# Attention ahead of two feed-forward layers: the order of its last steps, banks for the second queries, and the place of the block means

## The chip, the cores and the metric

The kernel runs on one core of a Trainium2 chip. The metric is the device time of one execution in microseconds (us); a run's time is compared by the median of several executions. Engines: PE multiplies matrices (PEld loads its weights), DVE, ACT and POOL work elementwise, SP issues the DMAs. Each engine runs its own list of instructions strictly in order and waits on semaphores for the others.

## What is computed

Three layers follow each other. The first is attention with 2 x 8 heads, 768 positions of 64 numbers, in which a query sees the keys nearer than 16 positions and, for each block of 32 positions, one summary (the maximum of the keys, the mean of the values):

```python
k_sum = k.reshape(B, H, nb, block, D).max(axis=3)
v_sum = v.reshape(B, H, nb, block, D).mean(axis=3)
scores_l = np.where(abs(i - j) < 16, scale * q @ k.T, -1e9)
scores_s = scale * q @ k_sum.T + np.log(block)
a = softmax(concatenate([scores_l, scores_s]))
x = a @ concatenate([v, v_sum])
x = (lambda h: h * np.cos(h))(x @ w_in) @ w_out          # 1536 x 512 -> 2048 -> 512
out = layernorm(h * softmax(h)) * g_ln @ w_out2          # h = x @ w_in2, 1024 wide
```

## The kernel before

The inputs are float32, or float64 read as pairs of words; here the weights come as pairs and are turned into float32 on the chip. Products of the feed-forward layers run in three passes over a high and a low part of each operand, so each weight tile is split into w[:, 0] and w[:, 1], and each input tile X into xs.

**Attention.** Heads go in 8 pairs n, each pair in 3 groups, 24 groups G = 3n + g of 4 query tiles of 64. One loop of 29 steps (L614) runs a software pipeline over the groups, and each engine's list is simply the order in which the loop emits: scores s(G) one step ahead (PE, L510, one bank for even and one for odd G), maximum and mask max(G) on DVE (L521), subtraction on POOL (L525), exp(G) a step later on ACT (L530), sum on DVE (L534), norm(G) two steps later on POOL (L540), the transposes T(G) of the weights four steps later on PE (L547, bank 2), their copy at(G) on ACT, or on DVE for the last four groups (L555, L553), the product with the values av(G) on PE (L567, bank 3), and x(G), the copy of its result into X (L581 on ACT, L579 on DVE from group 19 on). Even and odd steps are mirrored: av runs for two groups in every even step (L639), x for two groups in every odd step (L665).

**Pairs.** k(n) and q(n) are loaded by SP (L357; 384 KB each), set side by side (L375), transposed on PE into one tile of three banks (L443, L482), from which DVE takes the maximum of each key block, ksum (L455), and ACT copies the keys, kx (L464 to L474), and the queries, qx (L496). The first queries q(0) go to banks 2 and 3 and DVE copies them (L492). v(n) comes by four DMAs (L389, L393; 2 x 240 and 2 x 48 KB). vsum(n) on PE (L421) adds up each block of values, ACT scales the sums to means, vm(n) (L429), and SP places them by two DMAs into the rows of the v tile that av reads (L436). VSUM_AT says at which step vsum(n) stands, VLOAD_AT at which v(n) is loaded; the placing stood at the end of the step after vsum's, behind that step's loads (L688 to L694).

**Into the next layer.** While the attention runs, SP loads weights (raw, L139; 512 KB), and ACT and DVE (L163, L164, L171), then ACT and POOL (L186, L187) turn them into w. From step 15 on, FILL puts 48 products h of the first feed-forward layer (L234) between the attention's instructions on PE: four tiles h(0) to h(3). drain(k) emits what h needs behind it: u (ACT, L243), n (DVE, L248), sin (ACT, L253), h*r (DVE, L258), and the split gs (ACT L263, DVE L264). After the loop come the splits of X (L203, L204), then the products y(0), y(1) (L276) and from there an even alternation of h and y.

Of the kernel before, what the change touches and what calls it, by code (L numbers as in the profile page):

```python
# [34 lines left out]
def fused_kernel(  # L35
# [14 lines left out]
    nc = tc.nc  # L50
# [43 lines left out]
    WSTEPS = (4, 7, 10, 13, 16, 19, 20, 21)  # L94
    XS = (7, 11, 13, 17)
    IDLE = (0, 0, 0)
    DVE_AT = 20
    DVE_X = 19
    DVE_NORM = 99
    LAST = 5  # L100
# [205 lines left out]
            nc.tensor.matmul(t, lhsT=idle[:, 0:P], rhs=idle, start=True, stop=True)  # L306


    FILL = {15: 3, 16: 3, 17: 3, 18: 3, 20: 4, 21: 4, 22: 4, 23: 4, 24: 4, 25: 4, 26: 4, 27: 4, 28: 4}
    early = (x for step in range(GF) for x in h_products(step))  # L310

    def fill(step):
# [8 lines left out]

        nc.scalar.activation(out=small[:, 1:2], in_=small[:, 0:1], func=func)

    STAGES = ((emit_sin, 2), (emit_r, 2), (emit_u, 1), (emit_n, 1), (emit_g, 2))

    def drain(k):

        if k == 0:
            table(AF.Sin)
        for stage, at in STAGES:  # L330
            if 0 <= k - at < GF and (stage, k - at) != (emit_g, GF - 1):
                stage(k - at)


    def attention():
        st = ExitStack()
        with st:
# [24 lines left out]
            def load_q(n):  # L362
                q_t[n] = load_heads(q, n, "qt", NR)

            def load_k(n):
                k_t[n] = load_heads(k, n, "kt", 2)
# [17 lines left out]
            def load_v(n):  # L384
                b, hp = divmod(n, NP)
                t = io.tile([P, NT, 2, D], F32, tag="vt", name="vt", bufs=5)
                for j in range(2):
                    o = v[b, 2 * hp + j].offset
                    nc.sync.dma_start(  # L389
                        out=t[0:WIN, 1:NT - 1, j, :],  # L390
                        in_=bass.AP(v.tensor, o + (QT - BAND) * D, [[D, WIN], [QT * D, NT - 2], [1, D]]),
                    )
                    nc.sync.dma_start(  # L393
                        out=t[0:WIN, 0:NT:NT - 1, j, :],
                        in_=bass.AP(v.tensor, o, [[D, WIN], [(S - WIN) * D, 2], [1, D]]),
                    )
                v_t[n] = t
# [77 lines left out]
                    out=kx[:, :, WIN:KW], in_=ks_t.pop(n).unsqueeze(1).to_broadcast([P, NT, NS]), func=AF.Copy)  # L475

            def emit_q(n):
                if n == 0:
                    qk_t["q", n] = bank(2, "q0"), bank(3, "q1")
                t, (a, b) = q_t.pop(n), qk_t["q", n]  # L480
                for c in range(NR):
                    nc.tensor.transpose(  # L482
                        (a, b)[c // (NR // 2)][:, (c % (NR // 2)) * P:(c % (NR // 2) + 1) * P],
                        t[:, c].rearrange("p h d -> p (h d)"), ident)

            def emit_qx(n):
                qx = io.tile([P, S], F32, tag="qx", name="qx")
                rows = qx.rearrange("p (i r) -> p i r", r=NR)
                src = qk_t.pop(("q", n))
                if n == 0:  # L490
                    for r in range(2):
                        nc.vector.tensor_scalar_mul(  # L492
                            rows[:, :, r * NR // 2:(r + 1) * NR // 2],
                            src[r][:, 0:S // 2].rearrange("p (r i) -> p i r", i=P), 0.125)
                else:
                    nc.scalar.activation(  # L496
                        out=rows, in_=strided(src[0], 0, [[1, P], [P, NR]]), func=AF.Copy, scale=0.125)
                kx_t["q", n] = qx
# [50 lines left out]

            def emit_at(G):  # L550
                at = sm_p.tile([KW, NG, P], F32, tag="at", name="at", bufs=3)
                if G >= DVE_AT:
                    nc.vector.tensor_copy(at, at_t[G])  # L553
                else:
                    nc.scalar.activation(out=at, in_=at_t[G], func=AF.Copy)  # L555
                at_t[G] = at

            def emit_av(G):
                n, g = divmod(G, GPP)
                b, hp = divmod(n, NP)  # L560
                at, vt = at_t.pop(G), v_t[n]
                if G % 2 == 0:
                    o_t["bank"] = bank(3, "ops").rearrange("p (a i s) -> p a i s", a=2, i=NG)
                ops = o_t["bank"][:, G % 2]
                for i in range(NG):
                    for j in range(2):
                        nc.tensor.matmul(  # L567
                            ops[64 * j:64 * j + 64, i, :], lhsT=vt[0:KW, NG * g + i, j, :],
                            rhs=at[:, i, 64 * j:64 * j + 64], start=True, stop=True)
                o_t[G] = ops  # L570
# [17 lines left out]
            nc.sync.dma_start(out=mask.rearrange("p t k -> p (t k)"), in_=c_mask)  # L588
            load_k(1)
            load_q(1)  # L590
            load_k(2)
            load_q(2)
            load_v(0)
            nc.gpsimd.memset(small, 0.0)
            nc.gpsimd.memset(strip, 0.0)
            warm_up(8)
# [12 lines left out]


            LX, LN, LT, LA = 1, 2, 4, 5
            VSUM_AT = {3: 0, 4: 1, 7: 2, 9: 3, 12: 4, 13: 5, 16: 6, 19: 7}
            VLOAD_AT = {1: 1, 4: 2, 6: 3, 8: 4, 10: 5, 13: 6, 16: 7}
            for step in range(NGR + LA):  # L614
                n, g = divmod(step, GPP)
                summed = LN <= step < NGR + LN
                ahead = 1 if step == 1 else n + 1 if g == 0 and 0 < n < NPAIR - 1 else 0

                warm_up(IDLE[g] if step < min(FILL) else 0)
                odd = step % 2  # L620
                if step + 1 < NGR and not odd:
                    emit_s(step + 1)
                if odd and step in VSUM_AT:
                    sum_v(VSUM_AT[step])
                if step == 0:
                    pair_k(1)
                    emit_max(0)
                    pair_q(1)
                    emit_k(1)
                    emit_q(1)  # L630
                if LT <= step < NGR + LT:
                    emit_t(step - LT)
                if g == 2 and n + 2 < NPAIR:
                    emit_k(n + 2)
                    emit_q(n + 2)
                fill(step)
                if odd and step + 1 < NGR:
                    emit_s(step + 1)
                if not odd and step > LA:  # L639
                    emit_av(step - LA - 1)  # L640
                    emit_av(step - LA)
                if not odd and step in VSUM_AT:
                    sum_v(VSUM_AT[step])

                weights.split()
                if LX <= step < NGR + LX:
                    emit_exp(step - LX)
                if g == 1 and 0 < n < NPAIR - 1:
                    emit_kx_ends(n + 1)
                if summed:  # L650
                    emit_sum(step - LN)
                if ahead and step > 1:
                    emit_ksum(ahead)
                weights.rebias()
                if 0 < step < NGR:
                    emit_max(step)
                if step == 1:
                    emit_ksum(ahead)
                drain(step - NGR)
                if LT <= step < NGR + LT:  # L660
                    emit_at(step - LT)
                weights.finish()
                if summed:
                    emit_norm(step - LN)
                if step > LA and (odd or step == NGR + LA - 1):  # L665
                    end = step - LA + 1 - odd
                    emit_x(end - 2)
                    emit_x(end - 1)
                if ahead:
                    emit_kx(ahead)  # L670
                if step == 1:
                    emit_kx_ends(1)
                if step == 0:
                    emit_qx(1)
                if g == 2 and n + 2 < NPAIR:
                    emit_qx(n + 2)
                if step == 2:
                    weights.load(0)
                if step in WSTEPS:
                    weights.bits()  # L680
                for c in range(KC):
                    if step == XS[c]:
                        xs_of[0, c] = split_x(0, c, xs_a)
                if g == 1 and n + 2 < NPAIR:
                    pair_k(n + 2)
                    pair_q(n + 2)

                if g == 1 and n + 3 < NPAIR:  # L688
                    load_k(n + 3)
                    load_q(n + 3)  # L690
                if step in VLOAD_AT:
                    load_v(VLOAD_AT[step])
                if step - 1 in VSUM_AT:
                    place_vsum(VSUM_AT[step - 1])  # L694
                if step in VSUM_AT:
                    scale_v(VSUM_AT[step])

    with tc.manual_schedule():
# [200 lines left out]

        for c in range(KC):  # L900
            xs_of[1, c] = split_x(1, c, xs_b, nc.vector if c % 2 else nc.gpsimd)
        for k in range(LAST, 7):
            drain(k)
        emit_y(0)
        emit_y(1)
        for step in range(4, NSTEP):
# [93 lines left out]
```

## Time and profile before

| what | us |
|---|---|
| median of 3 runs | 493.17 (493.09 to 496.96) |
| the profiled execution | 493.84 |
| its span, first to last instruction | 492.0 |
| PE busy | 474.6 (96%) |
| ACT, DVE, POOL busy | 313.5, 302.7, 152.3 |

Only the span is profiled; 1.84 us of the profiled execution lie outside it. In a timeline row, the number behind the start is the duration, x8 is a count, and the bracket at the end says how long the engine had been idle before and which instruction ended that. fp32 products of the attention appear as two instructions each, so x16 is eight of the code's products. PEclk is TensorE's granted clock, 1.00 for 2.4 GHz.

### The profile page before, as it was taken

Reading aid. Unit: us, or ns where it says so; the run is one execution under the profiler, and the core shown is the slowest. Engines: PE = TensorE matmul, PEld = TensorE weight load, DVE = VectorE, ACT = ScalarE, POOL = GpSimd, SP = SyncE. Lnnn points to the kernel's source line nnn. Section 1 sums busy time; section 2 is a strip of 40 time slices with the busy share of each in tenths; the row PEclk is TensorE's granted clock in tenths of the full one; section 3 lists DMA queues with packets and bytes.
Section 4 is the critical chain, followed back from the end, with each engine's and each line's share of the span. In section 5 each row is a group of like instructions: output and inputs, shape, how many; then the busy total and the mean of one; then the engine's idle time right before and its main releaser. Section 6 shows DMA issues by size and latency. Waiting matters only on the chain.

```text
span 492.0 us, 7874 instructions
## 1 busy us (share of the span) xinstructions
PE 474.6 (96%) x2943; PEld 392.2 (80%) x2943; DVE 302.7 (62%) x666; ACT 313.5 (64%) x539; POOL 152.3 (31%) x146
## 2 busy tenths in 40 slices
PE   7789998899999999999999999999999999999997
PEld 4678877678888888888888888888888888888886
DVE  3698885783445446556474655556477766776661
ACT  2579877756686666656655653688624867777621
POOL 2388978722432223222322220245500011110000
PEclk9899999999999999999999999999999999999999
DMA  8888973201322332232223220220001333223211
GB/s 256 233 176 240 239 177 103 87 2 37 93 85 87 109 105 87 86 118 98 87 88 117 95 86 25 87 105 0 0 2 43 87 87 85 65 64 65 68 40 43
DMA packets 59046, 46.17 MB, mean 94 GB/s; under 512 B 40448, under 2 KB 51328, under 8 KB 59008
## 3 DMA queue, kind: packets, MB, share of 16 engines
q1 hardware_dynamic: 59008, 45.67, 32.5%
q8 instruction: 23, 0.38, 0.3%
q14 instruction: 15, 0.12, 0.1%
HBM read 36.61 MB, written 3.15 MB: 81 GB/s over the span
## 4 chain that ended last, share of the span: by engine, by line
PE 84%; ACT 4%; POOL 3%; DVE 3%; DMA 3%; issue 2%; SPq 1%; POOLq 0%; DVEq 0%; ACTq 0%
PE y L276 27%; PE h L234 24%; PE o L875 13%; PE h L761 13%; PE vsum L421 2%; POOL sm L525 1%; PE sps L510 1%; DMA qt<-in_q_dram 1%; POOL sm L540 1%; DMA vt<-in_v_dram 1%; PE aps L547 1%; PE ops L567 1%; ACT sm L530 1%; PE tp L809 1%; DMA vt<-vm 1%
## 5 line engine op out<-in xcount | busy, mean ns | idle before, releaser
L234 PE MATMUL h<-xs,w 128*128 128x512 f32 x576 | 141.2, 391 | 0.4 <-POOL xs L204 0.4
L276 PE MATMUL y<-gs,w 128*128 128x512 f32 x576 | 138.2, 389 | 0.0
L276 PEld LDWEIGHTS y<-gs,w 128*128 128x128 f32 x576 | 108.1, 188 | 22.5
L234 PEld LDWEIGHTS h<-xs,w 128*128 128x128 f32 x576 | 107.3, 188 | 22.3 <-POOL xs L204 0.7
L187 POOL TENSOR_TENSOR w<-s,w 128x512 fp32r<-128x512 f32 x48 | 62.1, 1295 | 155.8 <-ACT w L186 132.8
L243 ACT ACTIVATE r<-h 128x512 int32<-128x512 f32 x48 | 28.7, 597 | 85.7 <-PE h L234 85.7
L248 DVE SCALAR_TENSOR_TENSOR r<-r,h 128x512 f32<-128x512 int32 x48 | 33.0, 687 | 67.8 <-ACT r L243 67.6
L875 PE MATMUL o<-w,ls 128*128 128x512 f32 (+1 forms) x312 | 67.8, 374 | 0.0
L761 PE MATMUL h<-w,xs 128*128 128x512 f32 x288 | 67.6, 390 | 0.0
L171 DVE SCALAR_TENSOR_TENSOR s<-raw 128x512 int32<-128x512 int32 x48 | 37.1, 774 | 45.9 <-ACT raw L164 38.1
L875 PEld LDWEIGHTS o<-w,ls 128*128 128x128 f32 x312 | 55.3, 188 | 10.7 <-DVE ls L851 0.4
L761 PEld LDWEIGHTS h<-w,xs 128*128 128x128 f32 x288 | 53.9, 188 | 11.1
L204 POOL TENSOR_TENSOR xs<-X,xs 128x512 fp32r<-128x512 f32 x22 | 29.6, 1355 | 36.9 <-ACT xs L203 36.9
L796 POOL TENSOR_TENSOR st<-st,mhalf 128x1 f32<-128x1 f32 x12 | 6.6, 551 | 110.1 <-DVE st L795 101.7
L264 DVE TENSOR_TENSOR gs<-h,gs 128x512 fp32r<-128x512 f32 x48 | 32.7, 680 | 4.2 <-ACT gs L263 4.0
L253 ACT ACTIVATE r<-r,half_pi 128x512 f32<-128x512 f32 x48 | 34.5, 718 | 1.0 <-DVE r L248 1.0
L258 DVE TENSOR_TENSOR h<-h,r 128x512 f32<-128x512 f32 x48 | 32.9, 686 | 0.4 <-ACT r L253 0.4
L163 ACT ACTIVATE raw<-raw 128x512 f32<-128x512 f32 x48 | 31.9, 664 | 0.0
L164 ACT ACTIVATE raw<-raw 128x512 int32<-128x512 uint32 x48 | 31.8, 662 | 0.0
L186 ACT ACTIVATE w<-s 128x512 fp32r<-128x512 f32 x48 | 30.1, 628 | 1.8 <-DVE s L171 1.5
L525 POOL TENSOR_TENSOR sm<-sm,mx 128x480 f32<-128x480 f32 x24 | 26.0, 1083 | 15.2 <-DVE mx L521 15.2
L778 ACT ACTIVATE e<-h,st 128x1024 f32<-128x1024 f32 (+1 forms) x13 | 13.6, 1049 | 26.6 <-DVE st L774 23.2
(81 smaller groups left out, 560.4 us busy)
## 6 DMA issues: line engine op xcount, KB each, us to landing
raw<-in_moe_w_in_dram SPq DMA_DIRECT2D x24, 512.0 KB, 3.6
raw<-in_moe_w_out_dram SPq DMA_DIRECT2D x24, 512.0 KB, 3.3
vt<-in_v_dram SPq DMA_DIRECT2D x16, 240.0 KB, 5.8
kt<-in_k_dram SPq DMA_DIRECT2D x8, 384.0 KB
qt<-in_q_dram SPq DMA_DIRECT2D x8, 384.0 KB, 8.9
out_dram<-osb SPq DMA_DIRECT2D x11, 256.0 KB, 2.0
vt<-vm SPq DMA_DIRECT2D x16, 72.0 KB
vt<-in_v_dram SPq DMA_DIRECT2D x16, 48.0 KB, 4.5
```

Source lines behind the costliest of these rows:

```text
L163: nc.scalar.activation(out=hw, in_=hw, func=AF.Prelu, scale=REBIAS, alpha=NEGATIVE)
L164: nc.scalar.activation(out=lw, in_=lw.bitcast(U32), func=AF.Copy, scale=TOP3)
L171: nc.vector.scalar_tensor_tensor(out=self.f32[i], in0=t[:, :, 1], scalar=3, in1=t[:, :, 0], op0=ALU.logical_shift_left, op1=ALU.bitwise_or)
L187: nc.gpsimd.tensor_tensor(out=w[:, 1, :], in0=f, in1=as32(w[:, 0, :]), op=ALU.subtract)
L234: nc.tensor.matmul(h, lhsT=w[:, a, f * P:(f + 1) * P], rhs=xs_of[tb, c][:, b_, :], start=(m == 0), stop=(m == 3 * KC - 1))
L248: nc.vector.scalar_tensor_tensor(out=r, in0=r.bitcast(I32), scalar=TWO_PI, in1=h_of[step], op0=ALU.mult, op1=ALU.subtract)
L253: nc.scalar.activation(out=r, in_=r, func=AF.Sin, scale=-1.0, bias=half_pi)
L258: nc.vector.tensor_tensor(out=h, in0=h, in1=r, op=ALU.mult)
L264: nc.vector.tensor_tensor(out=gs[:, 1, :], in0=r, in1=as32(gs[:, 0, :]), op=ALU.subtract)
L276: nc.tensor.matmul(y[e], lhsT=w[:, a, e * P:(e + 1) * P], rhs=gs[:, b_, :], start=(f == 0 and i == 0), stop=(f == GF - 1 and i == 2))
L761: nc.tensor.matmul(banks[n], lhsT=xs_of[NTB + t // TPB, c][:, a, t0:t0 + P], rhs=weights.done[w2i[c][n]][:, b_, :], start=(m == 0), stop=( ...
L875: nc.tensor.matmul(o, lhsT=ls_of[t][f // 4][:, a, s0:s0 + P], rhs=w[:, b_, cols], start=(f == 0 and i == 0), stop=(f == NF2 - 1 and i == 2))
```

## The change

Seven edits, all in the attention and in what it overlaps with.

1. q(1) goes to banks 2 and 3 like q(0), and DVE copies it, in step 1 behind ksum(1).
2. v(0) is loaded ahead of k(2) and q(2), and vsum(0) stands in step 2 instead of 3.
3. The placing of vm(n) is emitted at the start of the step after vsum's, ahead of that step's loads.
4. FILL begins at step 16 instead of 15, and vsum(7) stands behind s(20) in step 19.
5. From step 24 on the steps are alike: av of one group in each, x of the same group at its end. av(20) to av(23) each use the first half of bank 3.
6. at stays on ACT for all groups and is emitted ahead of drain.
7. drain follows a table: u and n of h(0) and h(1) in steps 22 and 23, the others by the table, u, n, sin and h*r of h(3) after the loop.

```diff
-    FILL = {15: 3, 16: 3, 17: 3, 18: 3, 20: 4, 21: 4, 22: 4, 23: 4, 24: 4, 25: 4, 26: 4, 27: 4, 28: 4}
+    FILL = {16: 3, 17: 3, 18: 3, 19: 3, 20: 4, 21: 4, 22: 4, 23: 4, 24: 4, 25: 4, 26: 4, 27: 4, 28: 4}
...
-    STAGES = ((emit_sin, 2), (emit_r, 2), (emit_u, 1), (emit_n, 1), (emit_g, 2))
+    DRAIN = {
+        -2: ((emit_u, 0), (emit_n, 0)),
+        -1: ((emit_u, 1), (emit_n, 1)),
+        1: ((emit_sin, 0), (emit_r, 0)),
+        2: ((emit_sin, 1), (emit_r, 1), (emit_g, 0), (emit_u, 2), (emit_n, 2)),
+        3: ((emit_sin, 2), (emit_r, 2), (emit_g, 1)),
+        4: ((emit_g, 2),),
+        5: ((emit_u, 3), (emit_n, 3), (emit_sin, 3), (emit_r, 3)),
+    }
...
             def emit_q(n):
-                if n == 0:
+                if n < 2:
                     qk_t["q", n] = bank(2, "q0"), bank(3, "q1")
...
-                if n == 0:
+                if n < 2:
                     for r in range(2):
                         nc.vector.tensor_scalar_mul(
...
-                if G >= DVE_AT:
-                    nc.vector.tensor_copy(at, at_t[G])
-                else:
-                    nc.scalar.activation(out=at, in_=at_t[G], func=AF.Copy)
+                nc.scalar.activation(out=at, in_=at_t[G], func=AF.Copy)
...
-                if G % 2 == 0:
+                if G % 2 == 0 or G >= NGR - LT:
                     o_t["bank"] = bank(3, "ops").rearrange("p (a i s) -> p a i s", a=2, i=NG)
-                ops = o_t["bank"][:, G % 2]
+                ops = o_t["bank"][:, G % 2 if G < NGR - LT else 0]
...
             load_q(1)
+            load_v(0)
             load_k(2)
             load_q(2)
-            load_v(0)
...
-            VSUM_AT = {3: 0, 4: 1, 7: 2, 9: 3, 12: 4, 13: 5, 16: 6, 19: 7}
+            VSUM_AT = {2: 0, 4: 1, 7: 2, 9: 3, 12: 4, 13: 5, 16: 6, 19: 7}
...
+                if step - 1 in VSUM_AT:
+                    place_vsum(VSUM_AT[step - 1])
                 odd = step % 2
                 if step + 1 < NGR and not odd:
                     emit_s(step + 1)
-                if odd and step in VSUM_AT:
+                if odd and step in VSUM_AT and step < 19:
                     sum_v(VSUM_AT[step])
...
-                if not odd and step > LA:
+                if not odd and LA < step <= NGR:
                     emit_av(step - LA - 1)
+                if LA < step and (not odd or step > NGR):
                     emit_av(step - LA)
-                if not odd and step in VSUM_AT:
+                if step in VSUM_AT and (not odd or step == 19):
                     sum_v(VSUM_AT[step])
...
-                drain(step - NGR)
                 if LT <= step < NGR + LT:
                     emit_at(step - LT)
+                drain(step - NGR)
...
-                if step > LA and (odd or step == NGR + LA - 1):
-                    end = step - LA + 1 - odd
-                    emit_x(end - 2)
-                    emit_x(end - 1)
+                if LA < step < NGR and odd:
+                    emit_x(step - LA - 2)
+                    emit_x(step - LA - 1)
+                if step == NGR:
+                    emit_x(step - LA - 1)
+                if step >= NGR:
+                    emit_x(step - LA)
...
-                if step - 1 in VSUM_AT:
-                    place_vsum(VSUM_AT[step - 1])
```

Three places in the engines' lists. SP, steps 2 to 5, before: the first two weight loads, then k(4), q(4) and v(2), and behind them the placing of v(0) and v(1) together.

```order
L139 DMA raw<-in_moe_w_in_dram 128x1024 x2
L357 DMA kt<-in_k_dram 128x6x128
L357 DMA qt<-in_q_dram 128x2x384
L389 DMA vt<-in_v_dram 96x10x64
L393 DMA vt<-in_v_dram 96x2x64
L389 DMA vt<-in_v_dram 96x10x64
L393 DMA vt<-in_v_dram 96x2x64
L436 DMA vt<-vm 12x12x128 x4
L389 DMA vt<-in_v_dram 96x10x64
```

The same stretch after the change:

```order
L138 DMA raw<-in_moe_w_in_dram 128x1024
L442 DMA vt<-vm 12x12x128 x2
L138 DMA raw<-in_moe_w_in_dram 128x1024
L363 DMA kt<-in_k_dram 128x6x128
L363 DMA qt<-in_q_dram 128x2x384
L395 DMA vt<-in_v_dram 96x10x64
L399 DMA vt<-in_v_dram 96x2x64
L395 DMA vt<-in_v_dram 96x10x64
L399 DMA vt<-in_v_dram 96x2x64
L442 DMA vt<-vm 12x12x128 x2
```

The placing of v(0) stands between the two weight loads now, and that of v(1) alone ahead of v(3).

PE, steps 0 to 3, before (qk_209 holds k(1) and q(1), qk_268 the next pair; vsum_296 is vsum(0)):

```order
L443 MATMUL qk_209<-ident_73,kg_199 128x128 x6
L482 MATMUL qk_209<-ident_73,qg_207 128x128 x6
L510 MATMUL sps_224<-kx_167,qx_171 64x120 x8
L510 MATMUL sps_259<-kx_242,qx_222 64x120 x8
L443 MATMUL qk_268<-ident_73,kg_246 128x128 x6
L482 MATMUL qk_268<-ident_73,qg_248 128x128 x6
L421 MATMUL vsum_296<-vt_125,strip_110 64x128 x12
```

After the change:

```order
L449 MATMUL qk_209<-ident_73,kg_199 128x128 x6
L488 MATMUL q0_216<-ident_73,qg_207 128x128 x3
L488 MATMUL q1_217<-ident_73,qg_207 128x128 x3
L516 MATMUL sps_224<-kx_167,qx_171 64x120 x8
L516 MATMUL sps_262<-kx_242,qx_246 64x120 x8
L449 MATMUL qk_271<-ident_73,kg_249 128x128 x6
L488 MATMUL qk_271<-ident_73,qg_251 128x128 x6
L427 MATMUL vsum_284<-vt_121,strip_110 64x128 x12
```

q(1) is written to two tiles of its own; the order of s, k, q and vsum is the same here.

ACT, steps 22 and 23, before (raw and w are the weights, sm the exponentials, aps the transposes that at copies):

```order
L163 ACTIVATE raw_1321<-raw_1321 128x512
L164 ACTIVATE raw_1321<-raw_1321 128x512
L555 ACTIVATE at_1416<-aps_1375 120x512
L186 ACTIVATE w_1430<-s_1365 128x512
L530 ACTIVATE sm4_101<-sm4_101 128x4x120
L555 ACTIVATE at_1443<-aps_1420 120x512
L581 ACTIVATE X_75<-ops_1384 128x256 x2
L530 ACTIVATE sm5_102<-sm5_102 128x4x120
```

After the change (r is u, made from a tile h):

```order
L162 ACTIVATE raw_1326<-raw_1326 128x512
L163 ACTIVATE raw_1326<-raw_1326 128x512
L558 ACTIVATE at_1419<-aps_1378 120x512
L242 ACTIVATE r_1421<-h_1044 128x512
L185 ACTIVATE w_1436<-s_1368 128x512
L536 ACTIVATE sm4_101<-sm4_101 128x4x120
L558 ACTIVATE at_1449<-aps_1426 120x512
L242 ACTIVATE r_1451<-h_1288 128x512
L584 ACTIVATE X_75<-ops_1387 128x256 x2
L536 ACTIVATE sm5_102<-sm5_102 128x4x120
```

A u stands behind each of the two copies at, the first of them ahead of w and of the exponential behind it.

## Rows read from the trace of the kernel before

**Rows 1.** Windows: length, busy us PE, PEld, DVE, ACT, POOL, PEclk, DMA share, GB/s

```profile
18.00:20.00 2.00, 2.00 (x11) 2.00 (x10) 0.25 (x2) 0.00 (x0) 1.51 (x2) 0.50 1.01 235
...
110.00:120.00 10.00, 10.00 (x46) 8.29 (x45) 2.85 (x5) 4.75 (x9) 2.55 (x2) 1.00 0.00 0
```

**Rows 2.** Timeline of PE, steps 2 to 13: start us, us, engine, line, out<-in

```profile
16.67 1.04 PE L510 MATMUL sps<-kx,qx 64*64 64x120 f32 x16 [2.54 <-ACT kx L474]
17.64 1.54 PE L443 MATMUL qk<-ident,kg 128*128 128x128 f32 x6
...
20.39 1.82 PE L421 MATMUL vsum<-vt,strip 96*64 96x128 f32 x24
...
32.86 1.15 PE L567 MATMUL ops<-at,vt 120*64 120x64 f32 x32 [2.26 <-DMA vt<-vm]
33.81 1.51 PE L421 MATMUL vsum<-vt,strip 96*64 96x128 f32 x24
...
38.12 0.82 PE L443 MATMUL qk<-ident,kg 128*128 128x128 f32 x6
...
53.90 1.62 PE L421 MATMUL vsum<-vt,strip 96*64 96x128 f32 x24 [0.66 <-DMA vt<-in_v_dram]
```

**Rows 3.** Timeline of ACT, steps 0 to 9 and 22

```profile
13.20 0.81 ACT L496 ACTIVATE qx<-qk 128x768 f32<-128x768 f32 x1 [2.07 <-PE qk L482]
...
15.03 1.05 ACT L464 ACTIVATE kx<-qk 128x960 f32<-128x960 f32 x1 [0.53 <-DVE ksum L455]
...
44.54 0.31 ACT L429 ACTIVATE vm<-vsum 128x128 f32<-128x128 f32 x1
...
88.36 0.58 ACT L555 ACTIVATE at<-aps 120x512 f32<-120x512 f32 x1
89.81 0.63 ACT L186 ACTIVATE w<-s 128x512 fp32r<-128x512 f32 x1 [0.86 <-DVE s L171]
```

**Rows 4.** Timeline of DVE, steps 0 to 3 and 22 to 25

```profile
8.68 1.02 DVE L492 TENSOR_SCALAR qx<-q 128x384 f32<-128x384 f32 x2 [2.25 <-PE q L482]
...
14.04 0.96 DVE L455 TENSOR_REDUCE ksum<-qk 128x24 f32<-128x768 f32 x1 [1.40 <-ACT qx L496]
...
21.34 0.96 DVE L455 TENSOR_REDUCE ksum<-qk 128x24 f32<-128x768 f32 x1 [3.06 <-ACT qx L496]
...
88.50 1.27 DVE L171 SCALAR_TENSOR_TENSOR s<-raw 128x512 int32<-128x512 int32 x1 [0.70 <-ACT raw L164]
...
95.47 0.69 DVE L248 SCALAR_TENSOR_TENSOR r<-r,h 128x512 f32<-128x512 int32 x1 [1.13 <-ACT r L243]
```

**Rows 5.** Timeline of SP, which issues every DMA

```profile
19.60 0.92 SPq L139 DMA_DIRECT2D raw<-in_moe_w_in_dram  x2
...
28.60 3.73 SPq L436 DMA_DIRECT2D vt<-vm  x4
...
34.73 0.45 SPq L139 DMA_DIRECT2D raw<-in_moe_w_in_dram  x1
...
42.84 1.66 SPq L436 DMA_DIRECT2D vt<-vm  x2
44.61 0.46 SPq L139 DMA_DIRECT2D raw<-in_moe_w_in_dram  x1
...
51.83 1.66 SPq L436 DMA_DIRECT2D vt<-vm  x2
```

**Rows 6.** Timeline of PE, steps 19 to 28, and the first product behind them

```profile
76.68 1.60 PE L421 MATMUL vsum<-vt,strip 96*64 96x128 f32 x24 [1.24 <-ACT kx L471]
...
91.56 0.62 PE L547 MATMUL aps<-ident,sm 128*120 128x128 f32 x4 [0.90 <-ACT at L555]
...
96.90 0.62 PE L547 MATMUL aps<-ident,sm 128*120 128x128 f32 x4 [1.19 <-DVE at L553]
...
103.02 1.15 PE L567 MATMUL ops<-at,vt 120*64 120x64 f32 x32 [0.74 <-DVE X L579]
104.10 5.74 PE L276 MATMUL y<-gs,w 128*128 128x512 f32 x24
```

More of the change, by code (lines that the diff above doesn't have):

```diff
@@ L96, in fused_kernel @@
     IDLE = (0, 0, 0)
-    DVE_AT = 20
     DVE_X = 19
@@ L329, in drain @@
             table(AF.Sin)
-        for stage, at in STAGES:
-            if 0 <= k - at < GF and (stage, k - at) != (emit_g, GF - 1):
-                stage(k - at)
+        for stage, step in DRAIN.get(k, ()):
+            stage(step)
     def attention():
@@ L672, in attention @@
                     emit_kx_ends(1)
-                if step == 0:
                     emit_qx(1)
@@ L901, in fused_kernel @@
             xs_of[1, c] = split_x(1, c, xs_b, nc.vector if c % 2 else nc.gpsimd)
-        for k in range(LAST, 7):
-            drain(k)
+        drain(LAST)
         emit_y(0)
```

## Prediction

> **What bounds the kernel now.** I read the windows first, because they show where time can be won at all. From 104.10 us on, where PE begins y(0) [rows 6], PE has no gap: 10.00 of 10.00 us busy in 110 to 120 [rows 1], and the matmuls behind that point are the same in both kernels. So the change can only move the moment at which y(0) starts. The profiled execution took 493.84 us for a span of 492.0; what moves y(0) by x moves the time by x. I then followed PE through the attention and looked only at the rows with a wait. There are two families. Up to step 7, PE waits 2.54 us for ACT's kx before s(3), and then runs k(2), q(2) and vsum(0) at half the granted clock (0.50 in 18 to 20 us, that is 1.2 of 2.4 GHz); later it waits 2.26 us for the placed means of v(0) before av(0), and 0.66 us for the load of v(5) before vsum(5) [rows 1, 2]. From step 19 it waits 1.24, 0.90, 1.19 and 0.74 us for kx, for at on ACT, for at on DVE, and for X on DVE [rows 6]. Last I read SP, since two of the waits end with a DMA: SP has its queue of loads without a pause, and gets to the placing of v(0) and v(1) only at 28.60 us [rows 5].
>
> **The change part by part.**
>
> *Second queries in other banks.* ksum(1) on DVE stands idle 1.40 us until ACT has read q(1) out of the tile that k(1) shares with it; kx(1) on ACT waits for ksum(1), and s(3) for kx(1) [rows 2 to 4]. In banks of their own the queries don't hold ksum(1): 14.04 becomes 12.64, kx(1) and s(3) follow, s(3) starts at 16.67 - 1.40 = 15.27. Price: the copy of 0.81 us on ACT becomes two on DVE, 1.02 us together [rows 3, 4], right behind ksum(1): 12.64 + 0.96 + 1.02 = 14.6, before s(3) asks. Hidden.
>
> *The clock.* PE's pause before s(3) shrinks from 2.54 to 1.14 us. In the trace the low clock comes a microsecond after that pause; after the pause of 2.26 us at 32.86 it doesn't come (vsum 1.51 us at 33.81, against 1.82 at 20.39) [rows 2]. I take it that it stays away. k(2) falls from 1.54 to the 0.82 us of the k at 38.12, q(2), as long, likewise, vsum(0) from 1.82 to 1.51: 0.72 + 0.72 + 0.31 = 1.75 us. Bounds: 0 if the clock falls all the same, 1.75 if not.
> Together vsum(0) ends at 20.39 + 1.82 - 1.40 - 1.75 = 19.06. On the scores' side q(2) ends 1.40 + 1.44 = 2.84 us earlier, and with it qx(2), ksum(2) (21.34, it waits for that qx) and the DVE work behind it. I carry 2.8 us.
>
> *v(0) loaded before k(2) and q(2).* vsum(0) can stand in step 2 only with this. k(2) and q(2) land later by what four v transfers take. DVE's pair copies of them don't wait for a DMA in the trace, so the price is 0 as long as slack is left; at most it is the v share of a whole group (next paragraph), 576 of 1856 KB of 9.3 us, so 2.9 us. I take 0, since the copies now also stand behind the two qx, and keep 2.9 for the range.
>
> *Placing ahead of loads.* The place of v(0)'s means is now behind the first raw load, which SP issues at 19.60 at the latest, instead of at 28.60 [rows 5]. Its source vm(0) is done at 19.06 + 0.31 = 19.4 (a vm takes 0.31 [rows 3]). SP issues from 19.5, 1.66 us long, and av(0), which PE reaches at 32.86 - 2.26 - 2.8 = 27.8, no longer waits: 2.26 us saved on PE.
> What is late next? Everything on SP behind the placing: raw(1), k(4), q(4), v(2) start at 19.5 + 1.66 + 0.1 = 21.3. Such a group of raw, k, q and v took, from raw's issue at 44.61 to the start of the vsum that waited for it at 53.90, 9.3 us [rows 2, 5]. So v(2) is there at 30.6. PE is there at 27.8 + 0.95 (two av, 32.86 to 33.81) = 28.8 and waits 1.8 us: vsum(2) goes from 33.81 to 30.6, a gain of 3.2 us and not of 5.0.
> The same comes once more. The means of v(3) are now placed before raw(3), k(6), q(6), v(5). vm(3) ends at 44.54 + 0.31 - 3.2 = 41.65, all of ACT's work between hanging on PE's steps 7 to 9. From the placing's issue to raw(3)'s it takes 44.61 - 42.84 = 1.77, so raw(3) is at 43.4, v(5) at 52.7. PE would ask for it at 53.90 - 0.66 - 3.2 = 50.0. So the wait of 0.66 grows to 2.7 us, and vsum(5) starts at 52.7 instead of 53.90: of 3.2 us, 1.2 are left. With L for the 9.3, vsum(5) starts at 19.5 + 1.8 + L - 33.81 + 44.85 + 1.77 + L = 34.1 + 2 L. On SP such a group is issued in 7.2 us from 44.61 and in 8.1 from 34.73 [rows 5]; I carry the spread of 0.9 over to L, 8.5 to 10.2, and vsum(5) lies between 51.1 and 54.5.
>
> *Steps 13 to 22.* Here the distances hold, by the same rows, up to vsum(7). That stands behind s(20) now, with three products h in front, and its wait of 1.24 us is filled; the products taken out of step 15 buy nothing there, as s(17) waits for DVE. Net about 0.6 us. Then in step 22 the new u(0) on ACT and n(0) on DVE stand ahead of the weight's s (DVE, 88.50), for which ACT's w at 89.81 waits, and behind w the exp and at(19) that end PE's 0.90 us [rows 3, 4, 6]. at(18) ends at 88.94, u(0) takes as long as at, 0.58, n(0) 0.69: s would start at 88.94 + 0.58 + 0.69 = 90.2 instead of 88.50, so 1.7 later. s took 1.27 there beside POOL, and 0.6 to 0.7 of that may come back, as POOL then waits too. Bounds 0.4 and 1.7; I take 0.7. The gain so far is used up.
>
> *The plain steps.* at goes to ACT, av one group at a time, X right behind it. The waits of 1.19 and 0.74 us [rows 6] lose their cause: DVE has no at to copy and u, n of two steps are done before. But av(21), av(22) and av(23) share one bank now, each waits for the X before it, and that X stands on DVE behind the products of h, 0.69 us each. I give back 1.4 of the 1.93 us, so 0.5 is won. Bounds: 0 and 1.9.
>
> Sum: 1.2 + 0.6 - 0.7 + 0.5 = 1.6: 493.84 - 1.6 = 492.2. The median of the runs, 493.17, lies 0.67 below the profiled execution, so I forecast 491.6 us.
>
> The Trainium skill, DMA: Bandwidth & Descriptors, section Anatomy of one DMA, puts a transfer at about 2.0 us plus its bytes at 436 GB/s (fitted for transfers issued from GpSimd). By it, as an estimate, the group's 1856 KB would be there after 2.0 + 4.4 = 6.4 us, v(2) and v(5) before PE asks, and the result would be the first rival's. The group at 44.61 took 9.3, so the row decides.
>
> **Rivals.**
> 1. *The loads aren't late.* If L is below 28.8 - 21.3 = 7.5 us, neither vsum waits. For it: the queue was emptied earlier in the new order. Against it: SP alone needs 7.2 us to issue a group [rows 5]. Then some 4.6 us reach step 13 (DVE's s waits for ACT, which follows PE by 4.6), with 0.4 behind it 5.0: 488.2.
> 2. *Placing holds SP back (slower).* SP stands at the placing until the means are computed, with all loads behind it. If the v, k and q loads are late by half of the 2.9 us, raw(1) starts at 22.8; with L = 10.2, v(2) is there at 33.0, vm(3) at 44.05, raw(3) at 45.8, v(5) at 56.0, 2.1 us later than now; less the 0.4 behind, 1.7 slower: 493.17 + 1.7 = 494.9. It decides from L above 10.1 on, or from raw(1) 1.6 us later. For it: the group at 34.73 took 0.9 longer to issue.
> 3. *The clock falls anyway*, as PE still pauses 1.14 us, and once more 1.8 before vsum(2). Then vsum(0) and raw(1) come 1.75 later, vsum(5) starts at 54.45, 0.55 later than now, and with the 0.4 behind it the gain is used up: 493.3.
>
> **How the numbers follow.** Forecast 0.60, first rival 0.17, second 0.14, third 0.09. One per cent, 4.9 us, is about what a measurement of this kernel can tell from no change. Below 488.2 lies half of the first rival and a little of a better tail: 0.11. Above 498.1 only a pile of mishaps: 0.03. Within: 0.86. The range reaches from the first rival to the second, 488.2 to 494.9.
>
> **What would show it.** s(3) near 15.3 us; the clock at 1.00 throughout 15 to 24; av(0) without a wait; a wait of PE for v(2) before vsum(2), and for v(5) of 2 to 3 us before vsum(5), and SP waiting for vm ahead of raw; y(0) near 102.5. The forecast is wrong if no vsum waits for a load (first rival), or if vsum(5) starts after 53.9 (second).

## The result, and the profile after

The changed kernel takes 496.03 us (median of 20 runs, 492.12 to 498.19), the kernel before 493.13 us (20 runs, 491.20 to 496.96): ratio 1.0056, 95% interval 1.0033 to 1.0079. It is slower by about half a per cent, where 491.6 us and a small gain were forecast. The profiled execution took 493.28 us for a span of 491.5 us and is the second shortest of the 20; its granted clock (PEclk) is 0.996 on the mean of the execution, while the other runs lie between 0.988 and 1.000, with a median of 0.993. That difference will matter below.

The timeline of PE of the changed kernel, steps 2 to 14 (start us, us, engine, line, out<-in; to be read against [rows 2]). In the rows, sps are the scores s, qk holds k(n) and q(n), aps are the transposes T, ops the products av:

```profile
12.89 2.22 PE L516 MATMUL sps<-kx,qx 64*64 64x120 f32 x32
15.05 0.87 PE L449 MATMUL qk<-ident,kg 128*128 128x128 f32 x6
...
16.91 1.53 PE L427 MATMUL vsum<-vt,strip 96*64 96x128 f32 x24
...
27.46 1.15 PE L570 MATMUL ops<-at,vt 120*64 120x64 f32 x32
30.75 1.62 PE L427 MATMUL vsum<-vt,strip 96*64 96x128 f32 x24 [2.13 <-DMA vt<-in_v_dram]
...
48.78 1.48 PE L427 MATMUL vsum<-vt,strip 96*64 96x128 f32 x24
53.23 2.17 PE L427 MATMUL vsum<-vt,strip 96*64 96x128 f32 x24 [2.97 <-DMA vt<-in_v_dram]
55.34 1.11 PE L553 MATMUL aps<-ident,sm 128*120 128x128 f32 x4
56.38 2.42 PE L516 MATMUL sps<-kx,qx 64*64 64x120 f32 x32
```

The pause before s(3) is gone, k(2) takes 0.87 instead of 1.54 us, and av(0) at 27.46 waits for nothing: the two long waits of [rows 2] and the low clock behind the first are removed, as meant. Two others stand in their place. PE waits 2.13 us for v(2) and 2.97 us (0.66 before) for v(5). At vsum(4) the changed kernel is still 2.98 us ahead (48.78 against 51.76); at vsum(5) 0.67 us are left (53.23 against 53.90). The row of vsum(4) before:

```profile
51.76 1.48 PE L421 MATMUL vsum<-vt,strip 96*64 96x128 f32 x24
```

In the changed kernel, behind that second wait, every product is long: vsum 2.17 us where 1.62 is usual, the four aps 1.11 where 0.65, two s 2.42 where 1.86.

The windows of the same execution say why (length, busy us of PE, PEld, DVE, ACT, POOL, PEclk, DMA share, GB/s; to be read against [rows 1]):

```profile
18.00:20.00 2.00, 1.41 (x25) 1.00 (x20) 1.97 (x12) 1.51 (x3) 1.62 (x2) 1.00 1.09 266
...
52.00:54.00 2.00, 0.77 (x13) 0.80 (x15) 1.76 (x3) 0.53 (x2) 2.00 (x3) 1.00 0.71 101
54.00:56.00 2.00, 2.00 (x18) 1.67 (x15) 0.00 (x0) 0.00 (x0) 0.80 (x1) 0.54 0.99 329
56.00:58.00 2.00, 2.00 (x23) 1.66 (x23) 0.00 (x0) 1.49 (x4) 0.00 (x0) 0.61 1.08 321
58.00:60.00 2.00, 2.00 (x28) 1.84 (x25) 0.90 (x8) 2.00 (x5) 1.63 (x2) 1.00 1.13 261
```

The granted clock is 1.00 at 18 to 20 us, where it was 0.50 before. It now falls behind the wait for v(5): 0.54 and 0.61 in the four microseconds from 54 on, most of it at the lower of its two levels, 1.2 instead of 2.4 GHz. The three long products just named cost 0.55 + 0.46 + 0.56 = 1.57 us. So this execution has moved its low-clock stretch, not lost it.

SP's timeline shows where the waits come from (to be read against [rows 5]):

```profile
18.79 1.84 SPq L442 DMA_DIRECT2D vt<-vm  x2
20.67 0.52 SPq L138 DMA_DIRECT2D raw<-in_moe_w_in_dram  x1
...
26.21 2.18 SPq L399 DMA_DIRECT2D vt<-in_v_dram  x1
...
41.92 1.66 SPq L442 DMA_DIRECT2D vt<-vm  x2
43.68 0.47 SPq L138 DMA_DIRECT2D raw<-in_moe_w_in_dram  x1
```

And in the kernel before, the last transfer of v(2), just ahead of the placing at 28.60:

```profile
26.39 2.11 SPq L393 DMA_DIRECT2D vt<-in_v_dram  x1
```

The means of v(0) are placed at 18.79 instead of 28.60, and the loads of v(2) behind them are issued no earlier than before, the last at 26.21 against 26.39. SP gave away, by the placing, what the earlier work had won it, while PE comes to vsum(2) some five microseconds earlier (30.75 - 2.13 = 28.62 against 33.81). From raw(1)'s issue at 20.67 to vsum(2) at 30.75 it takes 10.1 us; from raw(3)'s at 43.68 to vsum(5), 9.55 us.

The chain of work that ended last, followed through this place (start us, us, what), says that this is now the path:

```profile
18.48 0.28 ACT vm L435
...
19.84 0.79 SPq L442
20.67 0.52 SPq L138
...
26.21 4.40 DMA vt<-in_v_dram
30.61 0.14 issue
30.75 1.62 PE vsum L427 x23
```

From the means of v(0) it runs through SP's placing, its queue of loads and the last transfer of v(2) to PE. In the kernel before, the means of v(0) were placed behind these loads.

PE's timeline from step 19 on (to be read against [rows 6]):

```profile
77.29 1.53 PE L427 MATMUL vsum<-vt,strip 96*64 96x128 f32 x24
...
91.36 0.63 PE L553 MATMUL aps<-ident,sm 128*120 128x128 f32 x4 [1.57 <-ACT at L558]
...
102.99 0.69 PE L570 MATMUL ops<-at,vt 120*64 120x64 f32 x16 [0.35 <-DVE X L582]
103.61 5.74 PE L275 MATMUL y<-gs,w 128*128 128x512 f32 x24
```

The wait for kx at vsum(7) is gone, the one for at has grown from 0.90 to 1.57 us, and y(0) starts 0.49 us earlier than before (103.61 against 104.10).

### The profile page after: what moved, and what is told of

Same layout as the page of the kernel before. It is cut to its first block, busy times and chain, and to the rows that moved or that the text cites. A ratio compares the mean times of both kernels' runs of the same rounds, so it can differ in the third digit from the quotient of the medians.

```text
span 491.5 us, 7871 instructions
## 1 busy us (share of the span) xinstructions
PE 476.3 (97%) x2943; PEld 392.7 (80%) x2943; DVE 300.5 (61%) x664; ACT 314.5 (64%) x542; POOL 151.6 (31%) x146
## 4 chain that ended last, share of the span: by engine, by line
PE 84%; ACT 4%; SPq 4%; DVE 3%; DMA 3%; issue 1%; POOL 1%; ACTq 0%; DVEq 0%; POOLq 0%
PE y L275 27%; PE h L233 25%; PE o L881 13%; PE h L767 13%; DMA vt<-in_v_dram 2%; SPq L399 2%; PE vsum L427 2%; PE aps L553 1%; DVE s L170 1%; DMA qt<-in_q_dram 1%; PE sps L516 1%; SPq L363 1%; PE ops L570 1%; POOL sm L531 1%; ACT raw L163 1%
## 5 line engine op out<-in xcount | busy, mean ns | idle before, releaser
L881 PEld LDWEIGHTS o<-w,ls 128*128 128x128 f32 x312 | 55.3, 188 | 10.7 <-DVE ls L857 0.4
L767 PEld LDWEIGHTS h<-w,xs 128*128 128x128 f32 x288 | 53.9, 188 | 11.1
```

Of the source, the lines that this page charges most:

```text
L767: nc.tensor.matmul(banks[n], lhsT=xs_of[NTB + t // TPB, c][:, a, t0:t0 + P], rhs=weights.done[w2i[c][n]][:, b_, :], start=(m == 0), stop=( ...
L881: nc.tensor.matmul(o, lhsT=ls_of[t][f // 4][:, a, s0:s0 + P], rhs=w[:, b_, cols], start=(f == 0 and i == 0), stop=(f == NF2 - 1 and i == 2))
```

## The experiments

Left open were the shares of three causes: the loads that now stand behind the placing, the clock that falls behind PE's waits, and the new order of the last steps. The ratios below are to runs of the kernel before that were taken beside each experiment.

**1. The placing back behind the loads** (the rest of the change kept).

```diff
-                if step - 1 in VSUM_AT:
-                    place_vsum(VSUM_AT[step - 1])
                 odd = step % 2
...
+                if step - 1 in VSUM_AT:
+                    place_vsum(VSUM_AT[step - 1])
                 if step in VSUM_AT:
                     scale_v(VSUM_AT[step])
```

> The changed kernel with its third edit undone: vm(n) is placed at the end of the step after vsum's, behind that step's loads, for all n. Queue theory (the placing ahead of loads holds v(2) and v(5) back; PE's long wait for v(5) uses up what the start won and lets the clock fall): v(5) is issued two placing DMAs, 1.7 to 1.8 us, earlier, PE's wait before vsum(5) falls from 2.97 to about 1.2 us, the clock stays at 1.00 around 54 to 57 us in most executions; time 0.6 to 0.9% below the changed kernel, so a ratio to before of 0.997 to 1.000. Rival 'v(0) first' (loading v(0) ahead of k(2), q(2) shifts the whole queue): the wait stays near 3 us, ratio 1.004 to 1.007. Rival 'steps' (the loss sits in steps 20 to 28): ratio 1.004 to 1.007, with a lower wait for v(5) but the same y(0).

Measured: 491.55 us, 0.9968 (0.9943 to 0.9994). The timeline of PE:

```profile
30.69 2.26 PE L427 MATMUL vsum<-vt,strip 96*64 96x128 f32 x24 [2.90 <-DMA vt<-in_v_dram]
...
50.29 1.48 PE L427 MATMUL vsum<-vt,strip 96*64 96x128 f32 x24
52.15 1.60 PE L427 MATMUL vsum<-vt,strip 96*64 96x128 f32 x24 [0.38 <-ACT vm L435]
```

SP in the same kernel:

```profile
18.79 1.84 SPq L442 DMA_DIRECT2D vt<-vm  x2
20.68 0.52 SPq L138 DMA_DIRECT2D raw<-in_moe_w_in_dram  x1
...
42.00 0.46 SPq L138 DMA_DIRECT2D raw<-in_moe_w_in_dram  x1
```

The wait for v(5) is gone and vsum(5) starts 1.1 us earlier than in the changed kernel. Without the third edit the change is a small gain: that edit costs 0.9% of the time (1.0056 against 0.9968). v(2) is late here as well, and SP shows why: with v(0) summed in step 2, its means are placed ahead of raw(1) even by the old rule, at 18.79 as in the changed kernel. So the second edit is enough for the wait for v(2) and for av(0) without a wait. The third makes v(5) later: raw(3), ahead of it in the queue, is issued at 42.00 here and at 43.68 in the changed kernel. That the whole wait of 2.97 us is the third edit's isn't shown, for PE also comes later here: vsum(4) starts at 50.29 instead of 48.78.

**2. Four v loads a step earlier** (on the changed kernel).

```diff
-            VLOAD_AT = {1: 1, 4: 2, 6: 3, 8: 4, 10: 5, 13: 6, 16: 7}
+            VLOAD_AT = {1: 1, 3: 2, 6: 3, 8: 4, 9: 5, 12: 6, 15: 7}
```

> The changed kernel with v(2), v(5), v(6) and v(7) loaded one step earlier, so that each stands ahead of a raw, k and q load; the placing stays ahead of loads. Queue theory: PE's waits for v(2) (2.13 us) and v(5) (2.97 us) shrink by what raw, k and q take in the queue, some 4 to 5 us, so both vanish, the clock doesn't fall; of the 3.4 us won by step 9 all reach step 13, and y(0) starts 4 to 6 us earlier than the changed kernel's typical one: ratio 0.988 to 0.993. Rival 'v(0) first': as the queue theory for the waits. Rival 'steps': the waits vanish but the time stays, ratio 1.002 to 1.006.

Measured: 489.42 us, 0.9915 (0.9884 to 0.9946), with a clock of 0.999 or 1.000 in every run. The timeline of PE:

```profile
27.80 1.54 PE L427 MATMUL vsum<-vt,strip 96*64 96x128 f32 x24
...
48.70 1.60 PE L427 MATMUL vsum<-vt,strip 96*64 96x128 f32 x24 [0.38 <-ACT vm L435]
...
99.72 5.73 PE L275 MATMUL y<-gs,w 128*128 128x512 f32 x24
```

No vsum waits for a load, vsum(5) starts 4.5 us earlier than in the changed kernel and y(0) 3.9 us earlier. One line of a table (v(2), v(5), v(6) and v(7), each a step earlier) turns the loss into a gain: the order of SP's queue decides whether PE waits, and with the waits the low clock is gone.

**3. The third edit alone on the kernel before.** The two lines of experiment 1 are moved the other way, and nothing else.

```diff
+                if step - 1 in VSUM_AT:
+                    place_vsum(VSUM_AT[step - 1])
                 odd = step % 2
```

> The kernel before with the third edit alone: vm(n) placed at the start of the step after vsum's, ahead of that step's loads. Queue theory: av(0) no longer waits 2.26 us, but v(5) stands behind two more placing DMAs and its wait grows from 0.66 to 2.5 to 3 us; ratio 1.000 to 1.006. Rivals 'v(0) first' and 'steps': the 2.26 us are won and nothing is lost, ratio 0.994 to 0.997.

Measured: 501.02 us, 1.0141 (1.0103 to 1.0179), worse than expected. The timeline of PE:

```profile
33.04 2.92 PE L421 MATMUL vsum<-vt,strip 96*64 96x128 f32 x24 [3.82 <-DMA vt<-in_v_dram]
...
57.30 1.62 PE L421 MATMUL vsum<-vt,strip 96*64 96x128 f32 x24 [2.16 <-DMA vt<-in_v_dram]
```

vsum(2) starts 2.3 us later than in the changed kernel and runs at half the clock (2.92 us). Behind it the reason, two rows of SP's timeline: with v(0) loaded and summed late, the placing is issued at 21.09 us (18.79 in the changed kernel), and SP, done with raw(0) at 19.29, stands there with all loads behind it.

```profile
18.84 0.45 SPq L139 DMA_DIRECT2D raw<-in_moe_w_in_dram  x1
21.09 1.83 SPq L436 DMA_DIRECT2D vt<-vm  x2
```

**4. The edits 4 to 7 alone on the kernel before** (FILL, vsum(7), at, the plain steps, the drain table).

```diff
-    FILL = {15: 3, 16: 3, 17: 3, 18: 3, 20: 4,
+    FILL = {16: 3, 17: 3, 18: 3, 19: 3, 20: 4,
...
-                drain(step - NGR)
                 if LT <= step < NGR + LT:
                     emit_at(step - LT)
+                drain(step - NGR)
```

> The kernel before with edits 4 to 7 alone: FILL from step 16, vsum(7) behind s(20), plain steps from 24 on, at on ACT throughout, and the new table of drain; the start and the placing are those of before. Queue theory: these edits win about 0.5 us or nothing, ratio 0.997 to 1.001. Rival 'steps': the loss is here, ratio 1.004 to 1.008. Rival 'v(0) first': as the queue theory.

Measured: 492.48 us, 0.9979 (0.9951 to 1.0006). The last steps are neutral or win a little; the loss isn't theirs. Its trace, that of the slowest of its 12 runs, shows something else:

```profile
31.36 1.15 PE L571 MATMUL ops<-at,vt 120*64 120x64 f32 x32 [0.47 <-DMA vt<-vm]
...
54.51 2.92 PE L428 MATMUL vsum<-vt,strip 96*64 96x128 f32 x24 [2.79 <-DMA vt<-in_v_dram]
```

Up to vsum(5) nothing is changed here against the kernel before, yet av(0) waits 0.47 us instead of 2.26 and vsum(5) 2.79 instead of 0.66. So these waits differ from execution to execution, and a late v(5) needs neither the second edit nor the third.

**5. PE kept busy in the two waits** (on the changed kernel): 9 products of zeros ahead of vsum(2), 13 ahead of vsum(5), into a tile that nobody reads. The loads and the queue stay as they are.

```diff
+                if step in (7, 13):
+                    warm_up({7: 9, 13: 13}[step])
                 if odd and step in VSUM_AT and step < 19:
                     sum_v(VSUM_AT[step])
```

> The changed kernel, with 9 products of zeros ahead of vsum(2) and 13 ahead of vsum(5), results unused: PE does something in the two waits for v(2) and v(5), as long as they last in the trace (some 1.9 and 2.8 us), and the loads come no earlier. It parts the two halves of the queue theory. If the falling clock makes the loss, the granted clock stays at 1.00 from step 7 on, vsum(5) starts as before at about 53.2 us, and the time falls by one to two clock falls of some 1.7 us each: ratio to before 0.998 to 1.001, with less spread. If the waits alone make it, the clock plays no part: ratio 1.004 to 1.008.

Measured: 493.43 us, 0.9999 (0.9972 to 1.0026); the 12 runs lie within 492.60 to 493.62, all with a clock of 0.999 or 1.000. PE's timeline, and the windows behind the second wait (the columns as above):

```profile
30.79 1.62 PE L427 MATMUL vsum<-vt,strip 96*64 96x128 f32 x24 [0.94 <-DMA vt<-in_v_dram]
...
50.68 2.96 PE L305 MATMUL idle<-idle 128*128 128x512 bf16 x12 [0.38 <-ACT vm L435]
54.40 1.62 PE L427 MATMUL vsum<-vt,strip 96*64 96x128 f32 x24 [0.75 <-DMA vt<-in_v_dram]
```

```profile
54.00:56.00 2.00, 1.60 (x25) 1.46 (x25) 0.00 (x0) 0.00 (x0) 0.85 (x1) 1.00 0.92 277
56.00:58.00 2.00, 2.00 (x33) 1.83 (x34) 0.27 (x3) 1.33 (x4) 0.00 (x0) 1.00 1.09 328
```

The loads land no earlier than in the changed kernel (30.79 and 54.40), yet the clock stays at 1.00 and 0.57% come back: 1.0056 - 0.9999, 2.8 us. This is about what the low clock costs the changed kernel. It is a difference of two ratios, each with an interval of some 0.25% to either side. The standing still itself is not given back here; experiment 2 takes both away and gains 0.84% more (0.9999 - 0.9915).

The 2.8 us are as many as the loss, but they aren't the whole cause of it, since the kernel before keeps its own stretches of low clock. The runs at like clock show it: at a mean clock of 0.993, nine runs of the changed kernel have a median of 496.04 us, and 15 of the kernel before (beside the experiments) one of 494.58. At 0.989 and 0.990, six runs of each, there is no difference (497.09 and 497.18). So up to half of the loss, 1.5 us by this estimate, may be there at the same clock; standing still for late loads would make it, but no run parts it. Three runs of the kernel before, beside experiment 5, show a clock of 1.000; they took 490.08 to 490.84 us, less than every run of experiment 5 and little more than experiment 2.

**6. The first edit alone on the kernel before** (the queries in other banks).

```diff
-                if n == 0:
+                if n < 2:
                     qk_t["q", n] = bank(2, "q0"), bank(3, "q1")
```

> The kernel before with the first edit alone: q(1) in banks 2 and 3, copied by DVE in step 1 behind ksum(1). Queue theory: s(3) starts 1.4 us earlier, PE's pause before it shrinks from 2.54 to about 1.1 us and the clock stays at 1.00 there in most executions, but av(0) then waits longer for the placing that SP reaches at 28.6 us, so little arrives at y(0): ratio 0.996 to 1.000. Rival 'the start counts by itself': 3 us arrive, ratio 0.993 to 0.995.

Measured: 493.53 us, 1.0002 (0.9976 to 1.0029). The timeline of PE:

```profile
14.10 1.04 PE L510 MATMUL sps<-kx,qx 64*64 64x120 f32 x16 [1.03 <-ACT kx L474]
...
29.96 1.71 PE L567 MATMUL ops<-at,vt 120*64 120x64 f32 x32 [3.22 <-DMA vt<-vm]
31.39 2.65 PE L421 MATMUL vsum<-vt,strip 96*64 96x128 f32 x24
```

s(3) waits 1.03 instead of 2.54 us, but av(0) waits 3.22 instead of 2.26 us for the placed means, with a low clock behind it (vsum 2.65 us). In this trace, that of a run 1.4 us quicker than the median, y(0) still starts earlier than before, at 102.49; in the medians nothing is won. Alone, the first edit moves the longest wait, and the low clock with it, to av(0).

**7. Placing late and v loads a step earlier** (both edits, of 1 and of 2, on the changed kernel).

> The changed kernel with v(2), v(5), v(6), v(7) loaded one step earlier and the placing behind the loads of its step: both remedies at once. Queue theory: PE's waits for v(2) and v(5) are gone already by the earlier loads, so putting the placing back changes nothing on PE as long as no av waits for the means: ratio 0.990 to 0.993, the same as with the earlier loads alone. If the placing ahead costs for another reason than the v loads, it is faster still by 1 to 3 us: 0.985 to 0.989.

Measured: 489.60 us, 0.9942 (0.9916 to 0.9968). That is a little more than the 0.990 to 0.993 expected if nothing changed on PE, and its interval overlaps that of experiment 2. Whether placing ahead of loads gains anything once the loads are early isn't settled; no cost of it is seen then.

**8. The v loads a step earlier on the kernel before** (the line of experiment 2 and nothing else).

> The kernel before with the loads of v(2), v(5), v(6) and v(7) a step earlier, nothing else. If the earlier loads pay only because the changed kernel lacks time for them (queue order), little comes here: PE has no wait at vsum(2) before, av(0) still waits 2.3 us for the placed means, and only the 0.66 us at vsum(5) go: ratio 0.997 to 1.001. If earlier v loads are a gain of their own, as large as on the changed kernel: 0.984 to 0.990.

Measured: 493.84 us, 1.0017 (0.9989 to 1.0045): nothing. In the medians, early loads are no gain of their own; on the changed kernel, where PE comes to vsum(2) some five microseconds earlier, they are (experiment 2). The wait of 2.3 us that was expected before av(0) isn't in its trace, that of the second quickest of the 12 runs: av(0) runs at 29.85 without a wait.

**9. The changed kernel without its second edit** (v(0) behind k(2) and q(2), vsum(0) in step 3).

```diff
             load_q(1)
-            load_v(0)
             load_k(2)
             load_q(2)
+            load_v(0)
...
-            VSUM_AT = {2: 0, 4: 1,
+            VSUM_AT = {3: 0, 4: 1,
```

> The changed kernel with its second edit undone: v(0) loaded behind k(2) and q(2), vsum(0) in step 3. If the early sum of v(0) is what lets SP place and go on to the loads, SP is held longer here, vsum(2) starts 0.5 to 2 us later than the 30.75 us of the changed kernel, and the ratio to the kernel before is 1.005 to 1.012. If k(2) and q(2) behind v(0) are what costs, vsum(2) starts earlier than 30.75 and the ratio is 0.998 to 1.003.

Measured: 497.23 us, 1.0076 (1.0049 to 1.0103). From the timeline of PE:

```profile
33.50 2.92 PE L427 MATMUL vsum<-vt,strip 96*64 96x128 f32 x24 [4.00 <-DMA vt<-in_v_dram]
```

In its trace vsum(2) starts 2.75 us later than in the changed kernel, a little more than expected, since SP places at 21.37 instead of 18.79. In the medians the difference is 1.2 us and the intervals overlap. So once means are placed ahead of loads, the second edit helps in the trace, and nothing shows that it costs.

**10. The drain behind the weights' own work** (on the kernel of experiment 2, against the 1.6 us wait for at in step 22).

```diff
-                drain(step - NGR)
                 weights.finish()
+                drain(step - NGR)
```

> The kernel with the earlier v loads, with drain emitted behind the weights' last DVE operation, so that in step 22 the weight's s no longer stands behind n(0) on DVE; nothing else moves. Step theory (u and n of h(0) ahead of s hold w, exp and at(19) back by about 0.7 us, seen as PE's wait of 1.57 to 1.63 us for at(19) where the kernel before waited 0.90): the wait falls to about 0.9 us and the time by 0.4 to 0.9 us against the kernel with the earlier v loads, ratio 0.988 to 0.991. If the wait comes from POOL's chain instead, it stays at 1.6 us and the ratio at 0.9915.

Measured: 488.68 us, 0.9905 (0.9872 to 0.9939). The timeline of PE:

```profile
87.21 0.63 PE L553 MATMUL aps<-ident,sm 128*120 128x128 f32 x4 [0.66 <-ACT at L558]
...
99.86 1.43 PE L275 MATMUL y<-gs,w 128*128 128x512 f32 x5
```

The wait falls from 1.63 us (in the trace of experiment 2) to 0.66, but y(0) starts at 99.86 against 99.72 there: the time isn't seen at the end of the attention. This is the quickest version of the study, 0.95% quicker than the kernel before; from experiment 2 it can't be told apart.

## Why the prediction was wrong

*What held.* The queries in other banks bring s(3) forward; in the changed kernel's trace s(3) follows s(2) without a pause, and experiment 6 shows it at 14.10 with 1.03 us of wait, against the 1.14 forecast. In the changed kernel av(0) waits no more. What is late next was named rightly, v(2) and v(5), though the sum laid both to the third edit, while for v(2) the second is enough (experiment 1), with vsum(2) at 30.75 (forecast 30.6) and vsum(5) at 53.23 (52.7). The wait of 2.97 us for v(5) was forecast as 2.7. The edits from step 13 on were put at +0.4 us. In the trace of experiment 5, where the clock doesn't fall, y(0) starts 49.38 us behind vsum(5) (103.78 - 54.40), against 50.20 before: 0.8 won. The wait in step 22 grew by 0.67 us, where I took 0.7; that it costs as much at y(0) isn't shown, since experiment 10 takes it away and y(0) doesn't move.

*What failed* is the step on the clock: "I take it that it stays away". I worked that step out for the pause before s(3) alone, where it is right, and set nothing against the two pauses of 1.8 and 2.7 us that the same forecast puts before vsum(2) and vsum(5). So the forecast has no low clock left in it. In the runs, the mean clock of the changed kernel is 0.993 on the median; that of the kernel before is 0.997 beside experiments 1 to 4 and again beside 8 and 9 (0.994 beside the others). Experiment 5 fills the two pauses and leaves the loads where they are; the low clock goes, and 2.8 us go with it, of the 4.4 by which the forecast missed (496.03 - 491.6). That the pauses come from SP's queue, experiments 1 and 2 show. The third rival had the mechanism ("once more 1.8 before vsum(2)"), but I priced it with the low clock of the start alone and set nothing against the pause for v(5), and gave it 0.09.

*How the sum misled.* I carried the distance of profiled execution and median, 0.67 us, over from the kernel before. In the changed kernel the median lies 2.75 us above the profiled execution, since that one is among the shortest of 20 and shows one low-clock stretch. Its y(0), 103.61, misses the forecast of 102.5 by 1.1 us; the rest of the error lies in the executions that no timeline here shows, and only their clocks speak for them.

*A term that was undersized* is L, the time from raw's issue to the vsum that waits behind it. I took 9.3 and a spread of 8.5 to 10.2. Measured: 10.1 and 9.55 us in the changed kernel; in experiment 5, 10.5 and 10.7 us (raw issued at 20.28 and 43.72, vsum(2) at 30.79 and vsum(5) at 54.40, the second 1.7 us later than forecast). Even with the clock held up the change is at 0.9999, where the forecast stood at 0.997 (491.6 of 493.17): 0.3%, 1.5 us, and this late v(5) is as large.

*The rivals.* The first (loads not late, 488.2 us) is what experiment 2 made true by another order of the queue: 489.42 us. The second (SP held back by the placing) is real where v(0) is summed late: experiments 3 and 9. In the changed kernel's trace SP isn't held up by the placing, as raw(1) is issued at 20.67, ahead of the 21.3 that I had. But its other condition, L above 10.1, is met in experiment 5, where vsum(5) starts past the 53.9 that I named as its sign; so loads later than forecast are part of the error even where SP doesn't stand.

*Not settled:* whether the placing ahead of loads is worth anything once loads come early (experiments 2 and 7 overlap), and how much the changed kernel loses at the same clock (nothing to 1.5 us, by the estimate under experiment 5), and in which waits.

## What to carry to other kernels

When a change takes a wait away and you name the wait that comes next, price the new one twice: the time PE stands still, and what PE runs at a lower clock behind it. An in-order queue that issues all loads makes every step forward of one entry a step back for those behind it, so move the loads whose consumer comes next along with it; that was worth 1.4% here, against 0.6% that the change lost. And where the runs of a kernel scatter by a per cent, read the mean clock of each run before you trust the one execution that was profiled.

## What the runs showed of the hardware

Like pauses were not always followed by the same clock. In the trace of experiment 4, s(3) took 1.86 us behind a pause of 2.54 us. In that of experiment 3, where the pause was 2.55 us, it took 1.04 us, which is usual, and vsum(0) behind it 1.53 us, which is usual too. The row of PE's timeline in experiment 4:

```profile
16.85 1.86 PE L517 MATMUL sps<-kx,qx 64*64 64x120 f32 x16 [2.54 <-ACT kx L481]
```

Two rows of the same view in experiment 3:

```profile
15.51 1.04 PE L510 MATMUL sps<-kx,qx 64*64 64x120 f32 x16 [2.55 <-ACT kx L474]
...
59.66 2.67 PE L510 MATMUL sps<-kx,qx 64*64 64x120 f32 x24
```

The last row is the s behind the 2.16 us wait of experiment 3 for v(5): 2.67 us for 24 instructions, where 32 take 1.86 at full clock. In the changed kernel's trace the 2.13 us before vsum(2) left the granted clock at 1.00 in the windows from 30 to 36 us. Over all traces, pauses of 2.1 to 2.6 us were followed by a low clock in some places and not in others; the six longer ones each time: 2.79 (experiment 4), 2.90 (experiment 1), 2.97 (the changed kernel), 3.22 (experiment 6), 3.82 (experiment 3) and 4.00 us (experiment 9). Part of the scatter of the runs goes with that: 492.12 to 498.19 us for the changed kernel, 492.60 to 493.62 with its two waits filled (experiment 5). Another part doesn't: the runs of experiment 7, all at 0.999 or 1.000, lie between 487.92 and 492.07 us.
